# Four more polynomial exponential tiles, and other orders at the start and the end, in a soft-capped attention with a soft mixture of experts

## The chip, the cores and the metric

The kernel runs on one core of a Trainium2 chip. The time is that of the device, in microseconds (us), for one launch; 8 runs of the kernel before are at hand. A core has five engines with queues of their own: PE (TensorE, matrix products and transposes, results in PSUM), ACT (ScalarE, functions of one argument), DVE (VectorE, elementwise), POOL (GpSimd) and SP (SyncE, here only DMAs). Within an engine, instructions run in the order of its queue; between engines they wait on semaphores.

## What is computed

```python
scores = cap * tanh((q @ k.T) / 8 / cap)        # 8 x 12 heads, 448 x 448, head_dim 64, cap 30
attn = exp(scores - max) / (sum(...) + 1e-9)
x = (attn @ v), heads side by side              # 3584 tokens x 768

logits = x @ phi                                # 3584 x 32 slots
d = softmax of logits over the tokens           # dispatch
slot_input = d.T @ x                            # 32 x 768, 4 slots for each of 8 experts
slot_out[e] = relu(slot_input[e] @ w1[e]) @ w2[e]   # 768 -> 1024 -> 768
c = softmax of logits over the slots            # combine
out = c @ slot_out                              # 3584 x 768, float32
```

## The kernel before

**Attention.** A pair is two heads of one batch; there are 48, two to a quad. Seven key tiles `c` of a pair make 336 tiles, each a column block of 448 scores over 128 partitions. A chunk `j` is six of them (`CH`), so there are 56 chunks (`NCH`), seven to a batch. `qk_chunk` (L283) puts half a chunk's scores into one of two PSUM tiles `sc`; `tanh_chunk` (L295) turns them into `ex` (ACT); `exp_part` (L304) takes the exponential in place (ACT). Since the cap bounds the scores, no maximum is subtracted. `pv_first` and `pv_rest` (L371, L388) multiply with the values and a column of ones, in a single PSUM tile with tag `pv`, and `norm` (L355) divides by the sum: a reciprocal and a multiply on DVE, which write `xq` and release that PSUM tile.

**Tiles of the exponential on DVE.** For a chunk in `shared` (L318), `exp_chunk` (L307) leaves tile 0 out, and `poly_exp` (L325) computes it on DVE in five steps (a scale and shift to a fixed-point power of two, the whole part as exponent bits, two steps of a polynomial in the fraction, the product), numbered 0 to 4. `PARTS` says after which slot of which chunk each step is queued, by `j % 7`. All share one scratch tile, `work`.

**The order of the work** is written out by hand. `at(j, slot, f, ...)` puts a job into slot `a`, `b`, `c`, `d`, `e` or `r` of chunk `j`, and `run(j, slot)` (L584) calls them; a `<` or `>` puts a job ahead of or behind the others of its slot. The main loop (L611) queues, for each chunk: two tanh, the exponential of the chunk before, `pv_first`, slot a, the scores of a half chunk, slot b, `pv_rest` (slot r between its reciprocal and multiply), slot c, the other scores, slot d. `spare`, `fill` and `busy` are matrix products of ones without use, which keep PE busy; `FILL` (L525) places those of every batch. Transposes of q, k and x, logits and small sums share the one PSUM tile with tag `T`.

**Start.** `first_half` (L223) brings q and k of the first pair into place: a cast to bf16, PE transposes (`turn`) into PSUM banks `one` and `two`, and copies out, in the order of the list at L231. `boots` are the two PSUM tiles that `sc` later uses.

**End.** After the loop (L646 on) come the last two pairs, the last logits, and the slot sums `slT` (L708). `e_norm` (L450) adds the dispatch weights of a batch to `zacc` (PE, DVE); of the last batch it runs at L772 and gives the factor `rz` that `relu` (L743) needs. `layer1` (L732) makes a half of the hidden layer for four experts, `h_transp` (L749) turns it into `hpad`, which `clear_hpad` (L516) has cleared on POOL (it lies in the memory of `work`), and `layer2` (L763) makes one half (384 columns) of the slot outputs `so`. The output is 28 pieces of 128 rows. While the second half of layer 2 runs, `half_tile` (L788) writes the first half of pieces 0 to 9 (`NH`); afterwards it writes their second halves, and the other pieces go out whole, two pieces to a store (L832 on).

Of the kernel before, what the change touches and what calls it, by code (L numbers as in the profile page):

```python
# [36 lines left out]
def kernel(  # L37
# [171 lines left out]
    def first_pieces(h, jobs):  # L209

        for stage, nm, c0, c1, eng, bank, at0 in jobs:
            copy = act.copy if eng is act else dve.tensor_copy
            cols = slice(h * HP, h * HP + HP)
            if stage == "cast":
                copy(casts[nm, 0][:, c0:c1, cols],
                     raws[nm, 0][h][:, c0 * DH:c1 * DH].rearrange("p (c d) -> p c d", d=DH))
            elif stage == "turn":
                for c in range(c0, c1):
                    pe.transpose(bank[cols, at0 + c - c0, :], casts[nm, 0][:, c, cols], ident)
            else:  # L220
                copy(qkT[nm, 0][cols, c0:c1, :], bank[cols, at0:at0 + c1 - c0, :])

    def first_half(h):  # L223
        for nm in ("k", "q"):
            if h == 0:
                qkT[nm, 0] = qk.tile([P, NT, P], BF16, name=nm + "T", tag=nm + "T")
        one = psT.tile([P, 8, P], BF16, name="ps1", tag="T")
        two = psV.tile([P, NT, P], BF16, name="ps2", tag="pv")
        if h == 0:

            first_pieces(h, (("cast", "k", 0, CS, dve, None, 0), ("cast", "q", 0, 4, dve, None, 0),  # L231
                             ("cast", "q", 4, NT, act, None, 0), ("turn", "k", 0, CS, pe, two, 0),
                             ("copy", "k", 0, CS, dve, two, 0), ("turn", "q", 0, 4, pe, one, 0),
                             ("cast", "k", CS, NT, act, None, 0),
                             ("copy", "q", 0, 4, dve, one, 0), ("turn", "q", 4, NT, pe, two, CS),
                             ("copy", "q", 4, NT, act, two, CS),
                             ("turn", "k", CS, NT, pe, one, 4), ("copy", "k", CS, NT, dve, one, 4)))
# [66 lines left out]
    def exp_part(j, u0, u1):  # L304
        act.activation(exs[j][:, u0:u1, :], exs[j][:, u0:u1, :], ACT.Exp, scale=cap)  # L305

    def exp_chunk(j):  # L307
        exp_part(j, 1 if j in shared else 0, CH)

    PARTS = {0: ((0, "a", (0, 1)), (0, "c", (2, 3)), (1, "<b", (4,))),
# [5 lines left out]
    shared = [j for j in range(NCH - 2) if j % 7 in PARTS and j > 5] if cap < 50 else []  # L318

    lead = POW2[0] / FRAC ** 3  # L320
    p2, p1, p0 = (c / POW2[0] * FRAC ** (n + 1) for n, c in enumerate(POW2[1:]))
    halves16 = xe.bitcast(U16).rearrange("p (s two) -> p s two", two=2)
    frac, whole = halves16[:, :, 0], halves16[:, :, 1]

    def poly_exp(j, ops):  # L325
        t = exs[j][:, 0, :]
        steps = (
            lambda: dve.tensor_scalar(xe, t, cap * math.log2(math.e) * FRAC,  # L328
                                      (127 + math.log2(lead)) * FRAC, ALU.mult, ALU.add),
            lambda: dve.tensor_scalar(xb.bitcast(U16), whole, 7, None, ALU.logical_shift_left),  # L330
            lambda: dve.scalar_tensor_tensor(xp, frac, p2, frac, ALU.add, ALU.mult),  # L331
            lambda: dve.scalar_tensor_tensor(xp, xp, p1, frac, ALU.add, ALU.mult),  # L332
            lambda: dve.scalar_tensor_tensor(t, xp, p0, xb, ALU.add, ALU.mult))  # L333
        for n in ops:
            steps[n]()

    def pv_mms(pr, c0, c1, gs, dst):

        Q, h = divmod(pr, 2)
        for tail in (False, True):  # L340
            for c in range(c0, c1):
                j, u = divmod(place[pr, c], CH)
                for g in gs:
                    if (g == NF) != tail:
                        continue
                    for n in range(2 if tail else 1):
                        r = slice(n * HP, n * HP + HP) if tail else slice(0, P)
                        q0, s0 = g * P, 2 * (g - gs[0])
                        out_, v_ = (dst[r, s0, :], vbds[Q % 2][r, h, c, n * W:n * W + W]) \
                            if tail else (dst[:, s0:s0 + 2, :], vbds[Q % 2][:, h, c, :])  # L350
                        pe.matmul(out_, exs[j][r, u, q0:q0 + (HP if tail else P)], v_,  # L351
                                  start=(c == 0 and g == gs[0] < NF), stop=(c == NT - 1),
                                  skip_group_check=True)

    def norm(pr, s0, s1, pv, between=()):  # L355
        Q, h = divmod(pr, 2)
        rec = xs.tile([P, NT, 1], F32, name="rec", tag="rec", bufs=4)[:, 0:s1 - s0, :]
        dve.reciprocal(rec, pv[:, 0:s1 - s0, DH:W])  # L358
        for f, a in between:
            f(*a)  # L360
        dve.tensor_tensor(xq[Q][:, h, s0:s1, :], pv[:, 0:s1 - s0, 0:DH],  # L361
                          rec.to_broadcast([P, s1 - s0, DH]), op=ALU.mult)

    def xq_tile(pr):
        Q, h = divmod(pr, 2)
        if h == 0:
            xq[Q] = xs.tile([P, 2, NT, DH], BF16, name="xq", tag="xq")
# [143 lines left out]
    def at(j, slot, f, *a):  # L511
        if j < 0:
            j, slot = 0, "b"
        aux.setdefault((j, slot), []).append((f, a))
# [7 lines left out]

        busy(n, psV.tile([P, P], F32, name="junk", tag="pv"))

    FILL = ((3, "a", fill, 2), (4, "a", fill, 2), (5, "a", fill, 2), (6, "a", spare, 10), (6, "c", spare, 14), (7, "a", fill, 24), (8, "a", fill, 8), (9, "a", fill, 2))  # L525
    PER = 2 * NQB * NT // CH
    assert PER == 7 and NQB == 3

# [10 lines left out]
    for b in range(B):  # L539
# [20 lines left out]
        if b < B - 1:  # L560
# [9 lines left out]
    for j in shared:  # L570
        for dj, slot, ops in PARTS[j % 7]:
            at(j + dj, slot, poly_exp, j, ops)
    for n, job in enumerate(wjobs):
        at(1 + n * (NCH - 5) // len(wjobs), "b", *job)
    for j, slot, n in ((0, "a", 10), (0, "c", 10), (1, "b", 10), (1, "c", 8)):
        at(j, slot, spare, n)
    for j, slot, n in ((NCH - 6, "d", 8), (NCH - 4, "d", 8), (NCH - 2, "d", 12)):
        at(j, slot, spare, n)
    at(NCH - 1, "a", clear_hpad)
    at(0, "c", init_vbd, 0)  # L580
    at(1, "c", init_vbd, 1)
    at(0, "d", vcast, 0)
# [28 lines left out]
    for j in range(NCH):  # L611
# [31 lines left out]
        run(j, "c")  # L643
        qk_chunk(2 * j + 3)
        run(j, "d")
    assert not aux, aux.keys()  # L646
    last, hpad = NPAIR - 1, hpads[0]
    assert place[last, 0] == NTILE - NT and pair_at[NCH - 3] == last - 2
    CL = CS
    exp_part(NCH - 1, 0, CL)  # L650
    exp_part(NCH - 1, CL, CH - 1)
    exp_part(NCH - 1, CH - 1, CH)
    attp.close()
# [10 lines left out]
    pv2 = [bank([P, 4, W], name=f"pvl{half}") for half in range(2)]  # L664
    junk = bank([P, P], name="junk")
    xq_tile(last - 1)
    for half, gs in enumerate(halves):
        pv_mms(last - 1, 0, NT, gs, pvm[half])
        norm(last - 1, cuts[half], cuts[half + 1], pvm[half])
        if half == 0:  # L670
            logits(NQ - 2)
    for half, gs in enumerate(halves):
        pv_mms(last, 0, NT - CH + CL, gs, pv2[half])
    x_transp(last - 1)
    for half, gs in enumerate(halves):
        pv_mms(last, NT - CH + CL, NT - 1, gs, pv2[half])
# [30 lines left out]
        js = slice(3 * s, 3 * s + 3)  # L707
        dve.tensor_tensor(slT[:, js, :], sl_ps[:, js, :], slacc[:, js, :], op=ALU.add)  # L708
    e_rep(bl)
    busy(8)  # L710
    att.close()


# [27 lines left out]
        return i, half, hp  # L741

    def relu(i, half, hp):  # L743
        if half == 0:
            act.activation(hbs[i][:, 0:512], hp, ACT.Relu, scale=rz)
        else:
            dve.tensor_scalar(hbs[i][:, 512:1024], hp, rz, 0.0, ALU.mult, ALU.max)

    def h_transp(i):  # L749

# [18 lines left out]
                      start=(n0 == 0), stop=(n0 == len(blocks) - 4))  # L769

    first = [layer1(0, half) for half in range(2)]
    e_norm(B - 1)  # L772
    for hp in first:
        relu(*hp)
    relu(*layer1(1, 0))
# [30 lines left out]
            act.mul(ob, home, winv[:, bb, c:c + 1])  # L806
        store(n, half, half + 1, ob)

    NH = 10
    so = [wts.tile([P, HD], BF16, name=f"so{half}", tag="w1", bufs=E) for half in range(2)]  # L810
    n2 = len(blocks)
    for n0 in range(0, n2, 4):
        if n0 == n2 // 2 - 8:
            h_transp(1)
        layer2(n0, 0)
    act.copy(so[0], so_ps[0])
    done = 0
    for n0 in range(0, n2, 4):
        layer2(n0, 1)

        if n0 % 8 == 4 and n0 != n2 // 2 + 4 and done < NH:
            for eng in ("act", "dve") if n0 < n2 // 2 else ("act",):
                half_tile(done, 0, bank([P, HD], name="op0") if done else
                          [bank([P, HD // 2], name="op00") for _ in range(2)], eng)
                done += 1
    dve.tensor_copy(so[1], so_ps[1])
    assert done == NH
    mid.close()


# [64 lines left out]
```

## Time and profile before

| What | us |
|---|---|
| median of 8 runs | 305.44 (305.16 to 305.85) |
| the profiled execution: its time | 305.36 |
| the profiled execution: its span, first to last instruction or transfer | 303.6 |
| first tanh starts | 6.98 |
| last exponential of the attention is queued in one row | 252.95 to 256.53 |
| layer 1, first matmul | 261.54 |
| first store of the output is issued | 272.25 |
| last compute on an engine ends | about 293.2 |

The page of a profile gives the busy time of each engine, then the span in 40 equal slices with a digit for the busy share in each, then DMA queues, the chain of work that ended last, and the costliest groups of instructions. The timeline lists instructions with start and duration in us, engine, line, operation, out<-in with shapes, a count where several are merged, and in brackets the idle time before it and what ended that. The chain of waits goes back from the last instruction, each piece to what released it. The table of windows gives, for a stretch A:B in us, the busy time and count of PE, PEld (weight loads), DVE, ACT and POOL, then the granted PE clock, the share of the DMA engines and GB/s. PEclk is the clock granted to PE, in tenths of full speed.

### The profile page before, as it was taken

To read this page: it belongs to the slowest core of one execution; us is meant where nothing else is said; L and a number is where in the kernel's file an instruction comes from. 1 tells how busy PE (TensorE), PEld (TensorE's weight loads), DVE (VectorE), ACT (ScalarE), POOL (GpSimd) and SP (SyncE) were. 2 spreads that over 40 slices of the span, in tenths; PEclk is the share of its full clock that TensorE was granted. 3 is DMA by queue.
4 is the path that set the end of the run, shared out by engine and by line. 5 is a ranking of instruction groups with operands and counts; after the bars stand their busy time and mean duration, and the time that the engine had idled before them with its cause. 6 is when DMAs were issued, how large, how long until landed. Compare 5 with 4: busy or idle time off the path is not lost.

```text
span 303.6 us, 10776 instructions
## 1 busy us (share of the span) xinstructions
PE 267.1 (88%) x4746; PEld 184.9 (61%) x4746; DVE 228.7 (75%) x493; ACT 269.0 (89%) x209; POOL 136.6 (45%) x176
## 2 busy tenths in 40 slices
PE   8898888999899989998999899999999999998820
PEld 7675656766666666666667566666666677642400
DVE  3714589889988999899879998999899845236840
ACT  4999999999999999999999999999999998236730
POOL 4483554385439534943394439443932260000000
PEclk9999999999999999999999999999999999999995
DMA  7999999799999999999899999999999649929997
GB/s 258 208 203 206 203 180 209 143 206 202 233 195 201 199 232 202 202 203 232 151 152 223 229 228 185 202 231 222 167 203 232 183 124 369 372 86 330 393 412 312
DMA packets 57486, 67.72 MB, mean 223 GB/s; under 512 B 3808, under 2 KB 53600, under 8 KB 57440
## 3 DMA queue, kind: packets, MB, share of 16 engines
q0 software_dynamic: 42448, 35.31, 75.2%
q1 hardware_dynamic: 14704, 31.50, 29.4%
q8 instruction: 37, 0.61, 0.8%
q10 hardware_dynamic: 288, 0.23, 0.2%
q14 instruction: 9, 0.07, 0.1%
HBM read 91.32 MB, written 18.87 MB: 363 GB/s over the span
## 4 chain that ended last, share of the span: by engine, by line
ACT 63%; PE 22%; DVE 7%; issue 4%; DVEq 0%; POOL 0%; ACTq 0%
ACT ex L301 34%; ACT ex L305 26%; PE pv L351 4%; PE sc L292 2%; PE so_ps L766 2%; PE hp L738 2%; PE junk L597 2%; PE op L846 2%; ACT ob L855 1%; PE boot L597 1%; PE op L802 1%; DVE xq L361 1%; ACT E L441 1%; DVE work L332 1%; PE pvl L351 1%
## 5 line engine op out<-in xcount | busy, mean ns | idle before, releaser
L301 ACT ACTIVATE ex<-sc 128x1344 bf16<-128x1344 f32 (+1 forms) x113 | 164.4, 1729 | 0.8 <-PE sc L292 0.8
L305 ACT ACTIVATE ex<-ex 128x2240 bf16<-128x2240 bf16 (+4 forms) x58 | 148.7, 2600 | 0.1
L351 PE MATMUL pv<-vbd,ex 128*128 128x130 bf16 (+1 forms) x1610 | 94.4, 211 | 8.9 <-DVE xq L361 6.3
L351 PEld LDWEIGHTS <-ex 128*128 128x128 bf16 (+1 forms) x1680 | 75.9, 101 | 29.2 <-issue 6.6
L292 PE MATMUL sc<-qT,kT 64*64 64x448 bf16 x672 | 69.6, 359 | 5.4 <-ACT ex L301 3.5
L270 POOL CAST vbd<-vraw 64x896 bf16<-64x896 f32 x23 | 21.9, 954 | 64.8 <-PE pv L351 43.9
L447 POOL COPY e<-E 128x512 bf16<-128x512 bf16 x9 | 5.5, 609 | 68.3 <-ACT E L441 34.6
L292 PEld LDWEIGHTS <-kT 64*64 64x64 bf16 x672 | 25.3, 104 | 12.5 <-issue 9.2
L332 DVE SCALAR_TENSOR_TENSOR work<-work 128x448 f32<-128x448 f32 x41 | 29.8, 727 | 0.7
L361 DVE TENSOR_TENSOR xq<-pv,rec 128x448 bf16<-128x448 f32 x46 | 28.7, 624 | 1.6
L331 DVE SCALAR_TENSOR_TENSOR work<-work 128x448 f32<-128x448 uint16 x41 | 28.9, 705 | 0.0
L410 DVE COPY xT<-xps 128x448 bf16<-128x448 bf16 x47 | 18.3, 389 | 12.8 <-PE xps L404 12.4
L333 DVE SCALAR_TENSOR_TENSOR ex<-work 128x448 bf16<-128x448 f32 x41 | 26.5, 646 | 0.6
L271 POOL CAST vbd<-vraw 64x896 bf16<-64x896 f32 x23 | 24.7, 1073 | 1.4
L110 POOL DMA_DIRECT2D w1b<-in_moe_w_dram x32 | 24.6, 771 | 0.0
L597 PEld LDWEIGHTS <-ones 128*128 128x128 bf16 x333 | 20.3, 102 | 6.2 <-issue 4.3
L597 PE MATMUL junk<-ones 128*128 128x128 bf16 x297 | 21.4, 220 | 0.8 <-DVE xq L361 0.3
L328 DVE TENSOR_SCALAR work<-ex 128x448 int32<-128x448 bf16 x41 | 20.6, 503 | 1.9 <-ACT ex L301 0.9
L262 DVE COPY kT<-kps 128x896 bf16<-128x896 bf16 x23 | 14.3, 621 | 8.9 <-PE kps L260 8.6
L182 POOL DMA_DIRECT2D kb<-in_k_dram x22 | 16.1, 733 | 7.3 <-PE kps L260 6.5
L182 POOL DMA_DIRECT2D qb<-in_q_dram x22 | 16.2, 736 | 3.6 <-DMA kraw<-in_k_dram 3.6
L358 DVE RECIPROCAL rec<-pv 128x7 f32<-128x7 f32 x46 | 9.3, 202 | 10.6 <-PE pv L351 10.5
(119 smaller groups left out, 345.5 us busy)
## 6 DMA issues: line engine op xcount, KB each, us to landing
w1b<-in_moe_w_dram POOLq DMA_DIRECT2D x32, 384.0 KB, 8.9
vraw<-in_v_dram SPq DMA_DIRECT2D x23, 448.0 KB, 5.4
w2d<-in_moe_w_dram POOLq DMA_DIRECT2D x20, 384.0 KB, 9.2
w2t<-w2d SPq DMA_DIRECT2D x20, 384.0 KB, 5.0
out_dram<-ob SPq DMA_DIRECT2D x8, 768.0 KB, 6.9
qb<-in_q_dram POOLq DMA_DIRECT2D x22, 224.0 KB, 9.0
kb<-in_k_dram POOLq DMA_DIRECT2D x22, 224.0 KB, 7.8
w2b<-in_moe_w_dram POOLq DMA_DIRECT2D x12, 384.0 KB, 9.0
```

The lines of the kernel that those rows point to most:

```text
L110: pool.dma_start(out=w1b[e][:, js, fs], in_=w1r[:, e, js, fs])
L182: (sp if nm == "v" else pool).dma_start(out=t, in_=quad_ap(nm, Q))
L271: pool.tensor_copy(t[HP:P, :, :, DH + 1:VW - 1], raw[HP:P])
L292: pe.matmul(sc[cs, u, 0:S], qkT["k", Q][r, c, cs], qkT["q", Q][r, :, cs], start=True, stop=True)
L301: act.activation(exs[j][:, half * CS + u0:half * CS + u1, :], sc[:, u0:u1, 0:S], ACT.Tanh, scale=qk_scale / cap)
L305: act.activation(exs[j][:, u0:u1, :], exs[j][:, u0:u1, :], ACT.Exp, scale=cap)
L331: lambda: dve.scalar_tensor_tensor(xp, frac, p2, frac, ALU.add, ALU.mult),
L332: lambda: dve.scalar_tensor_tensor(xp, xp, p1, frac, ALU.add, ALU.mult),
L333: lambda: dve.scalar_tensor_tensor(t, xp, p0, xb, ALU.add, ALU.mult))
L351: pe.matmul(out_, exs[j][r, u, q0:q0 + (HP if tail else P)], v_, start=(c == 0 and g == gs[0] < NF), stop=(c == NT - 1), skip_group_check= ...
L361: dve.tensor_tensor(xq[Q][:, h, s0:s1, :], pv[:, 0:s1 - s0, 0:DH], rec.to_broadcast([P, s1 - s0, DH]), op=ALU.mult)
L597: pe.matmul(junk if home is None else home, by, by, start=True, stop=True)
```

## The change

Tile 0 of chunks 3, 4, 5 and 53 is added to those that DVE computes (`EXTRA`), and steps of chunks with `j % 7` of 0, 1 and 6, and of 50 to 52, are queued at other slots. Two fills of each batch are shortened. At the start q's chunks 4 to 6 are cast, turned and copied first, in a PSUM bank of their own (`three`, in `boots[1]`). At the end `clear_hpad` is queued later, the last `e_norm` goes ahead of layer 1 in place of four useless products, the last `relu` is split between ACT and DVE, the copy of `so[0]` likewise, and pieces 10 and 11 join the half tiles (their first halves after the copy of `so[1]` is queued). The slots `t0` to `t2` hold no job.

```diff
         if h == 0:
 
-            first_pieces(h, (("cast", "k", 0, CS, dve, None, 0), ("cast", "q", 0, 4, dve, None, 0),
-                             ("cast", "q", 4, NT, act, None, 0), ("turn", "k", 0, CS, pe, two, 0),
-                             ("copy", "k", 0, CS, dve, two, 0), ("turn", "q", 0, 4, pe, one, 0),
-                             ("cast", "k", CS, NT, act, None, 0),
-                             ("copy", "q", 0, 4, dve, one, 0), ("turn", "q", 4, NT, pe, two, CS),
-                             ("copy", "q", 4, NT, act, two, CS),
-                             ("turn", "k", CS, NT, pe, one, 4), ("copy", "k", CS, NT, dve, one, 4)))
+            three = boots[1][:, CS - 1, :].bitcast(BF16).rearrange("p (c q) -> p c q", q=P)
+            first_pieces(h, (("cast", "q", 4, NT, act, None, 0), ("cast", "k", 0, CS, dve, None, 0),
+                             ("cast", "q", 0, 4, dve, None, 0), ("turn", "q", 4, NT, pe, three, 0),
+                             ("turn", "k", 0, CS, pe, two, 0), ("copy", "q", 4, NT, act, three, 0),
+                             ("turn", "q", 0, 4, pe, one, 0), ("copy", "k", 0, CS, dve, two, 0),
+                             ("cast", "k", CS, NT, act, None, 0), ("copy", "q", 0, 4, dve, one, 0),
+                             ("turn", "k", CS, NT, pe, three, 3), ("copy", "k", CS, NT, dve, three, 3)))
...
     def exp_chunk(j):
-        exp_part(j, 1 if j in shared else 0, CH)
+        exp_part(j, len(shared.get(j, ())), CH)
...
-    PARTS = {0: ((0, "a", (0, 1)), (0, "c", (2, 3)), (1, "<b", (4,))),
-             1: ((0, "<d", (0,)), (0, ">d", (1, 2, 3)), (1, "<b", (4,))),
+    PARTS = {0: ((0, "a", (0,)), (0, "<b", (1,)), (0, "c", (2,)), (0, "<d", (3,)), (0, ">d", (4,))),
+             1: ((0, "<d", (0,)), (0, ">d", (1, 2, 3)), (1, "a", (4,))),
...
-             6: ((0, "a", (0,)), (0, "<d", (1,)), (0, ">d", (2, 3)), (1, "<b", (4,)))}
-    shared = [j for j in range(NCH - 2) if j % 7 in PARTS and j > 5] if cap < 50 else []
+             6: ((0, "<b", (0,)), (0, "c", (1, 2)), (0, "<d", (3,)), (1, "a", (4,)))}
+    EXTRA = {3: (((0, "a", (0,)), (0, ">b", (1,)), (0, "<d", (2, 3)), (1, "a", (4,)),),), 4: (((0, "a", (0,)), (0, ">d", (1, 2)), (1, "<b", (3,)), (1, "r", (4,)),),), 5: (((0, ">b", (0,)), (0, "<d", (1,)), (0, ">d", (2, 3)), (1, "r", (4,)),),), 50: (((0, "<d", (0,)), (0, ">d", (1, 2, 3)), (1, "a", (4,)),),), 51: (((0, "<b", (0,)), (0, ">b", (1,)), (0, ">d", (2,)), (1, ">b", (3, 4)),),), 52: (((0, "c", (0, 1)), (0, "<d", (2,)), (0, ">d", (3, 4)),),), 53: (((0, "<b", (0,)), (1, "a", (1,)), (1, "<b", (2,)), (1, "<d", (3,)), (1, ">d", (4,)),),)}
+    shared = {j: (PARTS[j % 7],) for j in range(6, NCH - 6) if j % 7 in PARTS}
+    shared.update(EXTRA)
...
-    FILL = ((3, "a", fill, 2), (4, "a", fill, 2), (5, "a", fill, 2), (6, "a", spare, 10), (6, "c", spare, 14), (7, "a", fill, 24), (8, "a", fill, 8), (9, "a", fill, 2))
+    FILL = ((3, "a", fill, 2), (4, "a", fill, 2), (5, "a", fill, 2), (6, "a", spare, 10), (6, "c", spare, 12), (7, "a", fill, 18), (8, "a", fill, 8), (9, "a", fill, 2))
...
-    at(NCH - 1, "a", clear_hpad)
...
     for half, gs in enumerate(halves):
         pv_mms(last, 0, NT - CH + CL, gs, pv2[half])
+    clear_hpad()
...
     e_rep(bl)
-    busy(8)
+    busy(4)
+    e_norm(bl)
...
     def relu(i, half, hp):
-        if half == 0:
-            act.activation(hbs[i][:, 0:512], hp, ACT.Relu, scale=rz)
-        else:
-            dve.tensor_scalar(hbs[i][:, 512:1024], hp, rz, 0.0, ALU.mult, ALU.max)
+        f0, f1, mid = 512 * half, 512 * half + 512, 512
+        if i == half == 1:
+            mid = f0 + 288
+        if f0 < mid:
+            f2 = min(f1, mid)
+            act.activation(hbs[i][:, f0:f2], hp[:, 0:f2 - f0], ACT.Relu, scale=rz)
+        if mid < f1:
+            f2 = max(f0, mid)
+            dve.tensor_scalar(hbs[i][:, f2:f1], hp[:, f2 - f0:512], rz, 0.0, ALU.mult, ALU.max)
...
     first = [layer1(0, half) for half in range(2)]
-    e_norm(B - 1)
...
-    NH = 10
+    NH, NHL = 12, 10
...
-    act.copy(so[0], so_ps[0])
+    HB = HD // 2
+    act.copy(so[0][:, 0:HB], so_ps[0][:, 0:HB])
+    dve.tensor_copy(so[0][:, HB:HD], so_ps[0][:, HB:HD])
...
-        if n0 % 8 == 4 and n0 != n2 // 2 + 4 and done < NH:
+        if n0 % 8 == 4 and n0 != n2 // 2 + 4 and done < NHL:
...
     dve.tensor_copy(so[1], so_ps[1])
-    assert done == NH
+    for done in range(NHL, NH):
+        half_tile(done, 0, bank([P, HD], name="op0"), "dve" if done % 2 else "act")
```

More of the change, by code (lines that the diff above doesn't have):

```diff
@@ L316 @@
              5: ((0, "a", (0,)), (0, "c", (1,)), (0, ">d", (2,)), (1, "a", (3,)), (1, "<b", (4,))),
[1 row of a table removed]
-    shared = [j for j in range(NCH - 2) if j % 7 in PARTS and j > 5] if cap < 50 else []
[1 row of a table added]
+    EXTRA = {3: (((0, "a", (0,)), (0, ">b", (1,)), (0, "<d", (2, 3)), (1, "a", (4,)),),), 4: (((0, "a", (0,)), (0, ">d", (1, 2)), (1, "<b", (3,)), (1, "r", (4,)),),), 5: (((0, ">b", (0,)), (0, "<d", (1,)), (0, ">d", (2, 3)), (1, "r", (4,)),),), 50: (((0, "<d", (0,)), (0, ">d", (1, 2, 3)), (1, "a", (4,)),),), 51: (((0, "<b", (0,)), (0, ">b", (1,)), (0, ">d", (2,)), (1, ">b", (3, 4)),),), 52: (((0, "c", (0, 1)), (0, "<d", (2,)), (0, ">d", (3, 4)),),), 53: (((0, "<b", (0,)), (1, "a", (1,)), (1, "<b", (2,)), (1, "<d", (3,)), (1, ">d", (4,)),),)}
+    shared = {j: (PARTS[j % 7],) for j in range(6, NCH - 6) if j % 7 in PARTS}
+    shared.update(EXTRA)
+    if cap >= 50:
+        shared = {}
     lead = POW2[0] / FRAC ** 3
@@ L323, with poly_exp @@
     frac, whole = halves16[:, :, 0], halves16[:, :, 1]
-    def poly_exp(j, ops):
-        t = exs[j][:, 0, :]
+    def poly_exp(j, u, ops):
+        t = exs[j][:, u, :]
         steps = (
@@ L569 @@
                 at(*when("es"), e_sums, b // 2)
-    for j in shared:
-        for dj, slot, ops in PARTS[j % 7]:
-            at(j + dj, slot, poly_exp, j, ops)
+    for j, tiles in shared.items():
+        for u, parts in enumerate(tiles):
+            for dj, slot, ops in parts:
+                at(j + dj, slot, poly_exp, j, u, ops)
     for n, job in enumerate(wjobs):
@@ L645 @@
         run(j, "d")
-    assert not aux, aux.keys()
-    last, hpad = NPAIR - 1, hpads[0]
+    last = NPAIR - 1
     assert place[last, 0] == NTILE - NT and pair_at[NCH - 3] == last - 2
     CL = CS
-    exp_part(NCH - 1, 0, CL)
+    exp_part(NCH - 1, len(shared.get(NCH - 1, ())), CL)
     exp_part(NCH - 1, CL, CH - 1)
@@ L666 @@
     xq_tile(last - 1)
+    run(NCH - 1, "t0")
     for half, gs in enumerate(halves):
@@ L669 @@
         norm(last - 1, cuts[half], cuts[half + 1], pvm[half])
+        run(NCH - 1, f"t{half + 1}")
         if half == 0:
@@ L673 @@
         pv_mms(last, 0, NT - CH + CL, gs, pv2[half])
+    clear_hpad()
+    assert not aux, aux.keys()
+    hpad = hpads[0]
     x_transp(last - 1)
```

## The prediction

> **What bounds the kernel now.** I read the page first (busy shares, then the slices), then ScalarE's timeline, then the chain of waits, then a table of windows over the output. The page puts two engines level and cannot choose between them:
>
> ```profile
> PE 267.1 (88%) x4746; PEld 184.9 (61%) x4746; DVE 228.7 (75%) x493; ACT 269.0 (89%) x209; POOL 136.6 (45%) x176
> ...
> DVE  3714589889988999899879998999899845236840
> ACT  4999999999999999999999999999999998236730
> ...
> PEclk9999999999999999999999999999999999999995
> ```
>
> DVE has free tenths in slices 2 to 5 and again from slice 32: at the edges of the attention. ScalarE's timeline chooses:
>
> ```profile
> 85.67 2.75 ACT L301 ACTIVATE ex<-sc 128x1344 bf16<-128x1344 f32 x2
> 88.01 0.60 ACT L441 ACTIVATE E<-lg 128x128 bf16<-128x128 f32 x1
> 88.21 2.36 ACT L305 ACTIVATE ex<-ex 128x2240 bf16<-128x2240 bf16 x1
> 90.17 2.76 ACT L301 ACTIVATE ex<-sc 128x1344 bf16<-128x1344 f32 x2
> 92.51 2.75 ACT L305 ACTIVATE ex<-ex 128x2688 bf16<-128x2688 bf16 x1
> 94.84 2.78 ACT L301 ACTIVATE ex<-sc 128x1344 bf16<-128x1344 f32 x2
> ```
>
> Read starts, not durations: 88.21 to 90.17 is 1.96 us for a five-tile exp, 92.51 to 94.84 is 2.33 for a six-tile one, and these distances stay the same from 9.54 to 252.95 us with no idle entry. ScalarE is never starved. Recorded durations grow through the trace (the five-tile exp: 2.16 us at 40, 3.00 at 241), so ACT's start stamps run up to about 1 us early against the other engines; its ends fit them.
>
> At the end PE takes over, by the chain of waits:
>
> ```profile
> 246.00 0.62 PE sc L292 x6
> ...
> 248.55 0.79 PE junk L597 x12
> 249.34 0.04 issue
> 249.39 0.84 PE pv L351 x12
> ...
> 264.32 0.27 PE zps L455 x4
> ...
> 268.67 0.29 PE hps L755 x8
> ...
> 270.88 0.49 ACT so L816
> ```
>
> The scores at 245.87 start when the tanh of 243.60 has ended (245.82). Behind them PE runs with next to no gap to the last matmul of layer 2. After that the output's DMA is the limit:
>
> ```profile
> 278.00:280.00 2.00, 1.43 (x7) 0.56 (x6) 1.74 (x4) 1.63 (x4) 0.00 (x0) 1.00 0.65 227
> 280.00:284.00 4.00, 3.71 (x22) 1.76 (x22) 3.42 (x6) 3.58 (x5) 0.61 (x1) 1.00 1.04 370
> 285.00:294.00 9.00, 4.08 (x21) 1.82 (x19) 6.15 (x8) 4.93 (x6) 0.00 (x0) 1.00 1.02 415
> ```
>
> The last two columns are the DMA share and GB/s: full, except for a hole at 278 to 280.
>
> **1. Exponential tiles.** `shared` grows from 41 to 45 chunks: 3, 4, 5 and 53 are new. Each makes one exp five tiles wide instead of six: 2.33 - 1.96 = 0.37 us of ScalarE. Three early ones: **-1.12 us**, if PE and DVE follow. DVE pays five steps each (0.39 + 0.39 + 0.62 + 0.62 + 0.62 = 2.64 us); in 20 to 40 us it is busy 9.0 of 20. In its new order chunk 3's first two steps fall between the copy of qT (ends 21.17) and the next reciprocal (23.23). Chunk 4's last step goes between a reciprocal and the multiply of xq at about 32 us and holds xq, and the PSUM tile pv that PE reuses, by 0.55 us; PE has over 1.5 us until the tanh that releases its next scores (34.27), so this costs nothing. Were that cover gone it would cost its 0.55.
>
> What covers PE's lateness is the time from the last scores to their tanh: 0.48 us at its smallest recorded place in the loop's second half (235.48 to 235.97), 1.3 with ACT's early stamps put right. A shorter exp takes 0.37 of it.
>
> The fourth (chunk 53) falls into PE's own stretch. Its exp ends at 249.33, pv starts at 249.39; 0.37 earlier, PE is still in the 12 junk matmuls (until 249.34). DVE also finishes this tile late: its last two steps follow the copy of lg (248.55), so near 249.75, while pv reads it fourth of the pair, near 249.9. Ends: +0.2 (tile late) to -0.37 (all passes); I take **-0.10**, by the nearest row, PE's 0.04 us wait at 249.34.
>
> **2. Reordered steps (parts 0, 1, 6).** Same instructions, so no DVE time. Part 6 starts later in its chunk and ends sooner, parts 0 and 1 end sooner; behind the moved steps stand the copies of kT, qT and xT and the reciprocals, for whose PSUM tiles PE waits. Cover: the 1.3 us above. Cost 0; ends -0.3 and +4 (third rival).
>
> **3. Fewer fills.** 2 + 6 junk matmuls less per batch, 8 x 0.055 = 0.44 us. PE waits for ScalarE at the next scores, so nothing is gained. PEclk stays full at 20 to 40 us, where PE is busy only 17.16 of 20; the cut takes about 1.5 points from over 90%. Cost 0.
>
> **4. Start.** Now PE turns k, then q's first four chunks; q's last three wait for DVE's copy of kT, and ScalarE's copy of them (5.66, 0.47 us) is the last thing before the scores:
>
> ```profile
> 4.90 0.35 DVE L221 COPY kT<-ps 64x384 bf16<-64x384 bf16 x1 [0.42 <-PE ps L219]
> ...
> 5.22 0.42 DVE L221 COPY qT<-ps 64x512 bf16<-64x512 bf16 x1
> ...
> 5.66 0.47 ACT L221 COPY qT<-ps 64x384 bf16<-64x384 bf16 x1 [0.34 <-DVE qT L221]
> ...
> 6.19 1.32 PE L292 MATMUL sc<-qT,kT 64*64 64x448 bf16 x12
> ```
>
> After: q's three turns come first, in a bank of their own. Their cast ends at 4.10, PE can start at about 4.15 and pays 0.107 us each (its early spacing), so k's turns begin near 4.47 instead of 4.33: DVE's two copies slip 0.13, qT ends at about 5.77. ScalarE's copy runs at 4.71 to 5.18; its cast of the rest of k then slips from 4.92 to 5.18 and ends at 5.58; PE turns that k by 5.86, ahead of the scores in its queue. Scores at 5.87 instead of 6.19: **-0.32**; ends 0 (k's cast or its DMA late) and -0.5. The second scores still wait for DVE's copy of k, ready at 6.53 as before, and reach 7.34; their tanh comes at 7.9. Hidden.
>
> **5. From slots to layer 2.** Four junk matmuls and the four zps matmuls (0.22 + 0.27 us) now fill the wait for slT, where eight junk took 0.55: hidden, as long as POOL's e4 (ends 261.09) is not late. DVE's zacc sum and reciprocal (0.16 us each) go with them into DVE's idle time before 264.6. The 0.27 between the layer-1 halves goes. The relus no longer wait for rz (4.6 us on ScalarE), but what is late next is PE itself, so this gives no more. The last relu (DVE, 267.75, 0.75) held the transposes until 268.60 though PE had been free since about 268.4; split at 288 columns it takes about 0.50 on ScalarE (between 0.42 for 192 columns and 0.58 for 384), which removes that 0.2. **-0.47**; ends -0.2 and -0.6. clear_hpad moves behind id32 on POOL and waits for DVE's last step; from about 249.8 plus 1.8 it still ends 14 us before the first write to hpad. so[0] in two halves: 0.48 becomes about 0.36 (0.32 and 0.42 are the rows of 192 columns): **-0.12**; ends 0 and -0.2.
>
> **6. Two more early half tiles.** Before, the store issued at 276.89 is followed by the next at 278.37, since all wait for so[1]. Tiles 10 and 11 need only so[0]: their stores go out at about 277.5 and 278.0 and fill the hole, worth (370 - 227) / 370 x 2.0 = 0.77 us of DMA. Their other halves are small stores too: two tiles (0.79 MB) at 370 instead of 415 GB/s are 0.23 more. **-0.54**; ends +0.23 and -0.77. SP issues four small stores for one large, at 0.49 each, inside the 0.53 that each moves. The Trainium skill speaks against this step: "Perfetto Trace Analysis", DMA Optimizations, says that transfers under 2 KB carry a large overhead each and should be merged, and these rows are 1,536 bytes. "DMA: Bandwidth & Descriptors", Bandwidth, gives 0.95 us for 64 KB and 6.15 for 1 MB; my estimate between them for 192 KB is 1.7 us, so four stores would cost 6.8 where 0.79 MB at 415 takes 1.9: +4.9, and the change would be slower. The trace has the very store at 0.53 us, because the next is under way before one lands; I sum with that.
>
> **Sum:** -1.12 - 0.10 - 0.32 - 0.47 - 0.12 - 0.54 = -2.67 us. The profiled execution took 305.36 (span 303.6 and 1.76 around it), so 302.69; the runs' median 305.44 stands 0.08 above it. I forecast **302.7 us**.
>
> **Rivals.** (a) Partly hidden: the hole at 278 stays or moves, and start and relu give half. For it: DVE gets one more multiply just when so[1]'s first tiles come. Against: tiles 10 and 11 wait for nothing. 305.36 - 1.12 - 0.16 - 0.24 = **303.8**. (b) ScalarE's saving is eaten because PE, at 93% in the loop, cannot follow shorter chunks. For it: PE is late by over half a microsecond at chunks 52 and 53. Against: PE waits for ScalarE in nearly every earlier chunk. It keeps 4 to 6: **304.0**. (c) Slower: in the steady loop a reordered DVE step stands before a copy that PE needs, its 1.25 us (two steps at the end of part 0) pass the cover of 1.3 less 0.37, and ScalarE idles in each of the seven batches. It decides from 0.38 us a batch (2.67 / 7); at 0.6 it gives 305.36 - 2.67 + 4.2 = **306.9**. For it: DVE is 91% busy there. Against: the steps end sooner, not later. (d) Gains and losses cancel: 305.4.
>
> **Chances.** Forecast 0.60 (its own range 302.0 to 303.4), (a) 0.16, (b) 0.10, (c) 0.08, (d) 0.06. A change under 0.2% (0.6 us) cannot be told from none. Faster 0.86, same 0.06, slower 0.08. The range 301.9 to 304.5 takes in (a) and (b) and leaves out (c) and (d).
>
> **What would show it.** Five-tile exps 45 instead of 41, ScalarE's start distances unchanged and without idle entries; first scores near 5.9; scores of the last chunk near 244.4; no zps between the hp groups; 278 to 280 less 2.7 at full DMA rate. An idle entry on ScalarE between 20 and 250 us, PEclk under 9 in mid-run, or a pv waiting for DVE's last step would make it wrong.

## The result

The median after the change is **303.1 us** (302.86 to 305.39, 11 runs, ten of them at 303.38 or less) against 305.5 in 31 runs of the kernel before on the same chip; the ratio is 0.9928, with a 95% interval of 0.9917 to 0.9939. The profiled execution took 303.07, 2.29 less than that of before, and its span 301.3 is shorter by the same 2.29. The first rows of the page after:

```profile
PE 264.7 (88%) x4686; PEld 182.3 (61%) x4686; DVE 237.9 (79%) x515; ACT 267.8 (89%) x211; POOL 136.1 (45%) x176
...
DVE  3728989898998999899879998999899964336840
...
PEclk9999999999999999999999999999999999999995
```

ACT and PE are level as before; DVE's new steps stand in slices 3 to 5, where it had room. PEclk stays full. The exponential that gained can be read in ScalarE's timeline, by starts:

```profile
25.95 2.11 ACT L305 ACTIVATE ex<-ex 128x2240 bf16<-128x2240 bf16 x1
27.91 2.51 ACT L301 ACTIVATE ex<-sc 128x1344 bf16<-128x1344 f32 x2
...
86.93 2.36 ACT L305 ACTIVATE ex<-ex 128x2240 bf16<-128x2240 bf16 x1
88.89 2.76 ACT L301 ACTIVATE ex<-sc 128x1344 bf16<-128x1344 f32 x2
```

The same place before:

```profile
26.09 2.48 ACT L305 ACTIVATE ex<-ex 128x2688 bf16<-128x2688 bf16 x1
28.42 2.51 ACT L301 ACTIVATE ex<-sc 128x1344 bf16<-128x1344 f32 x2
```

The first of the new five-tile exps starts at 25.95 and is followed after 1.96 us; before, this place took 2.33. At 86.93 the distance is still 1.96, at the six-tile exp of 91.23 it is 2.33, and no row from 7 to 252 us has an idle entry: ScalarE still sets the pace.

The chain of waits at the end of the attention and through the last layers:

```profile
247.21 0.79 PE junk L601 x12
...
248.04 0.84 PE pv L355 x12
...
260.03 0.16 PE zps L459 x4
260.19 4.00 PE hp L747 x72
...
269.11 0.33 ACT so L830
269.46 0.37 DVE so L831
```

The sum `zps` now stands ahead of `hp`. The two halves of the copy of so[0] follow one another: VectorE starts when ScalarE has ended. Then the table of windows over the output, 1.6 us earlier than the windows shown of before:

```profile
276.40:278.40 2.00, 1.63 (x7) 0.57 (x6) 1.74 (x4) 1.69 (x3) 0.00 (x0) 1.00 1.04 367
278.40:282.40 4.00, 3.74 (x22) 1.68 (x20) 3.16 (x6) 3.32 (x5) 0.61 (x1) 1.00 1.03 366
283.40:292.40 9.00, 4.23 (x27) 2.00 (x26) 6.00 (x7) 4.39 (x5) 0.00 (x0) 1.00 1.02 409
```

The hole (227 GB/s) is gone. By stretches of the two traces, in us:

| Stretch | before | after | difference | forecast |
|---|---|---|---|---|
| start of the span to first tanh | 6.979 | 6.852 | -0.13 | -0.32 |
| to the last chunk's first scores | 238.886 | 237.669 | -1.22 | -1.12 |
| to the last chunk's pv | 3.521 | 3.520 | 0.00 | -0.10 |
| to layer 1 (`hp`) | 12.157 | 12.080 | -0.08 | 0 |
| `hp` to the first `hps` | 4.381 | 4.000 | -0.38 | -0.27 |
| first to second `hps` | 2.675 | 2.675 | 0.00 | -0.20 |
| to the copy of so[0] | 2.278 | 2.314 | +0.04 | 0 |
| copy of so[0] to the first store | 1.374 | 1.522 | +0.15 | -0.12 |
| first store to last transfer | 29.652 | 29.169 | -0.48 | -0.54 |
| last transfer to end of span | 1.682 | 1.494 | -0.19 | 0 |
| sum | 303.585 | 301.295 | -2.29 | -2.67 |

### The profile page after: what moved, and what is told of

Its sections match the earlier page's. It is cut to its first block, busy times and chain, and to the rows that moved or that the text cites. A ratio compares the mean times of both kernels' runs of the same rounds, so it can differ in the third digit from the quotient of the medians.

```text
span 301.3 us, 10670 instructions
## 1 busy us (share of the span) xinstructions
PE 264.7 (88%) x4686; PEld 182.3 (61%) x4686; DVE 237.9 (79%) x515; ACT 267.8 (89%) x211; POOL 136.1 (45%) x176
## 4 chain that ended last, share of the span: by engine, by line
ACT 64%; PE 20%; DVE 8%; issue 4%; POOL 1%; DVEq 0%; ACTq 0%
ACT ex L301 35%; ACT ex L305 26%; PE pv L355 4%; PE sc L292 2%; PE so_ps L780 2%; PE hp L747 2%; DVE xq L365 1%; PE op L862 1%; ACT ob L871 1%; PE boot L601 1%; PE op L815 1%; ACT E L445 1%; POOL vbd L270 1%; DVE work L335 1%; PE junk L601 1%
## 5 line engine op out<-in xcount | busy, mean ns | idle before, releaser
L305 ACT ACTIVATE ex<-ex 128x2240 bf16<-128x2240 bf16 (+4 forms) x58 | 147.0, 2571 | 0.1
L292 PE MATMUL sc<-qT,kT 64*64 64x448 bf16 x672 | 68.7, 359 | 4.9 <-ACT ex L301 3.8
L336 DVE SCALAR_TENSOR_TENSOR work<-work 128x448 f32<-128x448 f32 x45 | 32.7, 727 | 0.8
L335 DVE SCALAR_TENSOR_TENSOR work<-work 128x448 f32<-128x448 uint16 x45 | 31.9, 710 | 0.0
L337 DVE SCALAR_TENSOR_TENSOR ex<-work 128x448 bf16<-128x448 f32 x45 | 29.0, 644 | 0.7
L601 PEld LDWEIGHTS <-ones 128*128 128x128 bf16 x315 | 19.3, 102 | 6.6 <-issue 4.3
L601 PE MATMUL junk<-ones 128*128 128x128 bf16 x279 | 20.4, 220 | 1.1 <-DVE xq L365 0.8
L334 DVE TENSOR_SCALAR work<-work 128x448 uint16<-128x448 uint16 x45 | 18.6, 414 | 0.5
```

The costliest lines, as they stand in the source:

```text
L292: pe.matmul(sc[cs, u, 0:S], qkT["k", Q][r, c, cs], qkT["q", Q][r, :, cs], start=True, stop=True)
L601: pe.matmul(junk if home is None else home, by, by, start=True, stop=True)
```

## The experiments

Each is one edit of the kernel after, unless it says otherwise. Times are medians; the kernel before took 305.85, 305.48 and 305.52 us on the chip in the three groups, in the order told here. It differs by 0.37 between them, and the intervals of `so_whole`, `nh10`, `start_old` and `zps_late` overlap or touch that of the kernel after: what these four are worth is read from the stretches of their traces, and the medians only agree in direction.

**First group: four parts of the change, one at a time.** `no_tiles` computes tile 0 of chunks 3, 4, 5 and 53 on ScalarE again, `no_53` only that of chunk 53:

```diff
-    EXTRA = {3: (...), 4: (...), 5: (...), 50: (...), 51: (...), 52: (...), 53: (...)}
+    EXTRA = {50: (...), 51: (...), 52: (...)}                                  # no_tiles
+    EXTRA = {3: (...), 4: (...), 5: (...), 50: (...), 51: (...), 52: (...)}    # no_53
```

> The changed kernel without the four new exponential tiles (3, 4, 5, 53); the reordered steps, the shorter fills, start and end stay. Theory A (ScalarE's stream sets the time until PE's last stretch): the scores of the last chunk come 3 x 0.375 = 1.12 us later than in the changed kernel, and the time is 1.1 us longer, 304.2. Theory B (each exponential tile is worth its 0.37 wherever it lies): 1.5 us longer, 304.6. Theory C (PE's pace sets the loop and the reordered steps brought the gain): no longer than the changed kernel, 303.1.

> The changed kernel with the tile of chunk 53 given back to ScalarE. Theory A (behind the last chunk's scores PE sets the end): nothing changes after them; first matmul of layer 1 and time as in the changed kernel within 0.1 us, 303.1. Theory B: 0.37 us longer, 303.5.

`no_tiles` took 304.23 (ratio 0.9951, 0.9937 to 0.9965), 1.13 over the kernel after; `no_53` took 303.12 (0.9915, 0.9901 to 0.9928). The two ran in one group and differ by 1.11, so the three early tiles give the whole 1.1, and the fourth nothing. The trace of `no_tiles` agrees: from 50 us on its exps start 1.12 later, counted from the first tanh, than in the kernel after (until the clock falls at 92 us; see the end). The last chunk's pv follows its scores by 3.52 us before, after and in `no_53` alike: the twelve junk matmuls stand between, whenever the exp ends.

`so_whole` copies so[0] in one piece again:

```diff
-    act.copy(so[0][:, 0:HB], so_ps[0][:, 0:HB])
-    dve.tensor_copy(so[0][:, HB:HD], so_ps[0][:, HB:HD])
+    act.copy(so[0], so_ps[0])
```

> The changed kernel with so[0] copied by ScalarE in one piece. Theory A (the two halves of the split copy run one behind the other, since DVE's half waits for ScalarE): last matmul of layer 2's first half to the first whole op matmul shrinks from 0.9 to about 0.75 us, and the first store comes 0.15 us earlier; time 302.9 to 303.0. Theory B (the split saves a third of the copy, as its shorter rows say): 0.1 us longer, 303.2.

It took 302.80 (0.9904, 0.9891 to 0.9918), and its copy to first store 1.374 instead of 1.522. The split costs 0.15: two serial copies of 0.32 and 0.36 us with a hand-over, 0.71 in all, for one of 0.48; 0.08 is won back, since the first of the two products of piece 0 is made earlier. (The median fell by 0.30, more than expected; the intervals touch.)

`nh10` takes back the two early half tiles:

```diff
-    NH, NHL = 12, 10
+    NH, NHL = 10, 10
```

> The changed kernel with ten early half pieces as before instead of twelve. Theory A (the two more fill the hole in the output's transfers): the hole of about 0.7 us between the store of the tenth half piece and the next comes back, and the time is about 0.5 us longer, 303.6. Theory B (small stores cost what merging would save, and the hole is hidden by the transfers behind it): no longer, or shorter by up to 0.2.

It took 303.90 (0.9942, 0.9928 to 0.9957), 0.8 over the kernel after, for an expected 0.5. Two terms in the trace: the hole is back (first store to last transfer 29.648), and behind the last transfer the span ends after 1.68 us instead of 1.49. There SP passes one wait after another on the stores, 0.06 us each: eight behind the last transfer in `nh10` and before, five in the kernel after.

**Second group: what was still open.** `start_old` has before's list of first pieces; `fills_old` has before's numbers of fills; `zps_late` has eight junk matmuls ahead of layer 1 again and `e_norm` between its halves; `tail_free` changes several places of the tail together.

> Only the order of the first pieces is put back; all else as after the change. Theory A (the new order of turns is worth something, but less than 0.32 us where the granted clock rises late, since the ten turns before the first scores run at half clock until then): first scores at 6.1 to 6.3 us if the clock rises near 5, later than after's 6.06 at a later rise; time 303.1 + 0.2 to 0.4, so 303.3 to 303.5. Rival (the order is worth nothing, the moment of the clock's rise alone sets the first scores): time 303.1 within 0.1, and first scores at the same clock rise as early as with the new order (5.65 to 5.8 for a rise before 4.2 us).

It took 303.38 (0.9938, 0.992 to 0.9955), 0.28 more than after. The granted clock rose at 6.70 us in its trace and at 5.68 in that of after, so the first scores (6.37 and 6.06) are not to be compared alone. With the new order, profiles with a rise at 3.40, 4.16, 5.10 and 6.17 have their first scores at 5.65, 5.81, 6.02 and 6.24 (another with a rise at 3.51 has 5.76, so 0.1 is scatter); the old order in before's trace had 6.19 with a rise at 4.95. So both matter: the order by some 0.2 at nearly the same rise, the rise by up to 0.6.

```diff
-    busy(4)
-    e_norm(bl)
+    busy(8)
...
     first = [layer1(0, half) for half in range(2)]
+    e_norm(B - 1)
```

> Only the place of the last batch's sum is put back: eight junk matmuls in the wait for slT, and zps, sum and reciprocal between the layer-1 halves. Theory A (the move is worth 0.44: 0.27 of zps, 0.11 because the first relu and so the transposes no longer wait for the reciprocal, 0.06 because the eight junk matmuls had held the layer-1 matmuls): layer 1 starts 1.38 to 1.40 us after the last slpl instead of 1.383 or so with 0.06 more, hp to hps 4.38 instead of 4.00, time 303.1 + 0.44 = 303.55. Rival (the prediction: only the 0.27 of PE): hp to hps 4.27, time 303.35.

303.50 (0.9939, 0.9927 to 0.9951): 0.40 more. `hp` to the first `hps` is 4.381 again, and layer 1 starts 1.449 after the last slot products begin, instead of 1.383. By these two stretches the move is worth 0.45, more than the 0.27 of its matmuls on PE.

```diff
-    ... (6, "c", spare, 12), (7, "a", fill, 18), (8, "a", fill, 8), ...
+    ... (6, "c", spare, 14), (7, "a", fill, 24), (8, "a", fill, 8), ...
```

> Only the fill matmuls are put back to 14 and 24 (8 more per batch, 0.44 us of PE in each of seven batches). Theory A (ScalarE sets the pace, fills are free both ways): last chunk's scores as many us behind the first as after the change (238.46), time 303.1 within 0.15. Rival 1 (the cut was needed, since PE must follow shorter exps): later by up to 7 x 0.44 = 3 us, at least 0.5. Rival 2 (the cut lets the granted clock fall now and then, which cost 0.9 us in one profile): the median is lower by 0.2 or more.

304.07 (0.9955, 0.994 to 0.997): 0.97 more. Theory A fell; rival 1 has the number, but the trace denies its reason: from the first scores to the last chunk's it takes 238.468 us, and in the kernel after 238.463. All of it lies in the output: first store to last transfer 30.10 instead of 29.17. The windows and SP's timeline of `fills_old` there, and its DMA packets by queue from 276.9 to 277.9 (count, MB, share of the time of the 16 DMA engines):

```profile
276.30:277.80 1.50, 1.31 (x5) 0.38 (x4) 1.24 (x3) 1.39 (x3) 0.00 (x0) 1.00 1.04 363
...
278.30:278.80 0.50, 0.46 (x3) 0.10 (x1) 0.45 (x2) 0.46 (x1) 0.00 (x0) 1.00 0.06 9
```

```profile
277.11 1.48 SPq L796 DMA_DIRECT2D out_dram<-obh  x1
```

```profile
q1 hardware_dynamic: 255, 0.35, 96.5%
q8 instruction: 1, 0.02, 6.4%
```

One store's issue lasts 1.48 us. Its counterpart in the kernel after, at the same place behind the first store, lasts 0.41:

```profile
277.40 0.41 SPq L796 DMA_DIRECT2D out_dram<-obh  x1
```

The pieces of output are written at the same distances from the first store in both traces, so no tile was late. Meanwhile the DMA runs dry (9 GB/s). The other thing there is queue q8, one packet of 16,384 bytes at 277.17: a load of instructions. Its 6.4% of 16 engines' one us is 1.0 us, where a packet of q1, which carries the stores, takes 0.06 on average; the two stores issued in that stretch landed 3.9 us after their issue, those of the kernel after 2.1. In every profile 36 or 37 such packets lie on q8, some 7.3 us apart on average. That they are PE's code is inferred from their number: PE has 4,686 matmuls and as many weight loads; 36 loads for 9,372 instructions are one per some 260. The Trainium skill ("Runtime: NRT & Kernel Launch", Instruction fetch mechanics) says that engines stream their code in blocks of 16 KiB, 256 instructions, and calls the crossing mostly hidden. In the kernel after, the last load comes at 269.31, ahead of the first store, and no other follows. With 56 matmuls and their weight loads more, PE is further on in its code at every moment: the last two loads come at 266.75 and 277.17, and the latter is among the stores.

`tail_free` copies so[0] and the last relu whole, cuts the junk, and queues chunk 53's steps earlier:

```diff
-    for j, slot, n in ((NCH - 6, "d", 8), (NCH - 4, "d", 8), (NCH - 2, "d", 12)):
+    for j, slot, n in ((NCH - 6, "d", 8), (NCH - 4, "d", 8), (NCH - 2, "d", 1)):
...
-    53: (((0, "<b", (0,)), (1, "a", (1,)), (1, "<b", (2,)), (1, "<d", (3,)), (1, ">d", (4,)),),)
+    53: (((0, "<b", (0,)), (1, "a", (1,)), (1, "<b", (2, 3)), (1, "<c", (4,)),),)
...
-        if i == half == 1:
-            mid = f0 + 288
```

> From after: so[0] copied whole by ScalarE, the last layer-1 relu whole again on VectorE, 1 junk matmul instead of 12 before the last pv, and the fourth tile's VectorE steps moved one or two slots earlier. Theory A (the fourth exponential tile's 0.37 us is hidden only by the 12 junk matmuls on PE; the relu split gave nothing; the split copy cost 0.15): first pv of the last chunk follows its scores by 3.15 us instead of 3.52; the two groups of hps stay 2.675 apart; time 303.1 - 0.37 - 0.15 = 302.6. Rival 1 (behind the junk VectorE or another wait takes over): distance stays 3.4 to 3.5 and the time is 302.8 to 302.95. Rival 2 (the relu split did help, as the prediction has it): hps groups 2.87 apart, time 302.8 at best. Rival 3 (without the junk the clock falls or a bank is not free): over 303.1.

303.39 (0.9933, 0.9921 to 0.9944): none of the four. Up to the first store all went as theory A has it: from the last chunk's first scores to the beginning of the last slot products 13.85 us instead of 14.22 (pv comes 0.61 earlier, 0.25 of which is lost again behind it), the two `hps` groups 2.675 apart, copy to first store 1.372. But the output took 29.81, and again one store's issue was long, 1.05 us at 270.38, with a load of code at 269.99.

**Third group: the load of code (theory C) against its rivals.** If the load is the cause, its place is set by the number of PE instructions ahead of it. Then 14 fills fewer should cost time, 126 more should cost none, and 14 put back should mend `tail_free`.

```diff
-    ... (6, "c", spare, 12), (7, "a", fill, 18), (8, "a", fill, 8), ...
+    ... (6, "c", spare, 14), (7, "a", fill, 24), (8, "a", fill, 18), ...    # fills_more
+    ... (6, "c", spare, 12), (7, "a", fill, 16), (8, "a", fill, 8), ...     # fills_less
+    ... (6, "c", spare, 14), (7, "a", fill, 18), (8, "a", fill, 8), ...     # tail_page: tail_free with this
```

> From after: 18 fill matmuls more per batch (2 and 6 as in the kernel before, and 10 more in another slot), 126 in all, close to the 128 matmuls (256 PE instructions with their weight loads, 16 KB) that lie between two of PE's code loads. Theory C (the 0.97 us of the old fills is no time of PE: PE's code load of 16 KB came at 277.17, among the small stores, held one issue on SP for 1.48 us instead of 0.40 and emptied the DMA; with 126 more it falls where it fell in after, ahead of the first store): last load at 269 to 270, first store to last transfer 29.1 to 29.3, time 303.1 within 0.2, faster than the kernel with 56 more. If PE's slack in the loop does not hold 1 us more, the distance from first to last scores grows over 238.47, and the output still takes 29.2. Rival (fills cost PE time that the shorter exps need): more fills, more time: 304.5 or over.

> From after: 14 fill matmuls fewer (18 to 16 in one slot, seven batches). Theory C (PE's code load): with 14 fewer the last load slips by over 1 us, to about 271, among the first stores, holds one issue on SP for about 1 us, and first store to last transfer becomes 29.7 to 30.2: time 303.6 to 304.0, slower with fewer instructions. Rival (fills cost PE time, or nothing): 303.1 or less, output 29.2.

> tail_free (so[0] whole, relu whole, 1 junk for 12, tile 53's steps earlier) with 14 matmuls put back as fills in the loop (12 to 14 in one slot, seven batches), so that PE's last code load falls ahead of the first store again. Theory C: no store's issue on SP over 0.45 us before the large ones, first store to last transfer 29.1 to 29.3 instead of 29.81, time 302.5 to 302.7 (303.1 - 0.37 for the fourth tile - 0.15 for the whole copy), the fastest of all. Rival (tail_free's output was longer for another reason: SP's third store waited for a slower tile): 303.2 to 303.4 again.

| Kernel | PE matmuls | load of code nearest the stores | first store issued | longest issue of a small store | first store to last transfer | time |
|---|---|---|---|---|---|---|
| before | 4746 | 277.24 | 272.25 | 0.41 | 29.65 | 305.5 |
| nh10 | 4686 | 269.80 | 270.91 | 0.42 | 29.65 | 303.90 |
| after | 4686 | 269.31 | 270.63 | 0.41 | 29.17 | 303.1 |
| fills_old | 4742 | 277.17 | 270.33 | 1.48 | 30.10 | 304.07 |
| fills_more | 4812 | 269.24 | 270.73 | 0.41 | 29.14 | 303.19 |
| fills_less | 4672 | 273.27 | 272.99 | 1.29 | 30.05 | 304.15 |
| tail_free | 4675 | 269.99 | 269.89 | 1.05 | 29.81 | 303.39 |
| tail_page | 4689 | 269.32 | 270.14 | 0.42 | 29.15 | **302.56** |

Fewer fills are slower, and 126 more are not told apart from the kernel after (0.09). Theory C held in all three. The traces bear it out on PE's own count. Matmuls and weight loads that PE has begun when the last load comes, in the table of windows from the start of the span on, for the kernel after, `fills_less` and `fills_old`:

```profile
0.00:269.31 269.31, 247.99 (x4558) 175.65 (x4558) 221.54 (x490) 253.52 (x190) 135.47 (x175) 1.00 1.09 211
0.00:273.27 273.27, 251.16 (x4557) 177.11 (x4557) 220.75 (x493) 254.60 (x191) 136.61 (x175) 0.99 1.07 207
0.00:277.17 277.17, 256.51 (x4689) 179.40 (x4690) 225.61 (x500) 258.40 (x199) 136.79 (x175) 1.00 1.08 212
```

The five kernels of the table with 36 loads have 4,557 to 4,562 matmuls behind them there, the three with 37 have 4,684 to 4,689, one load or some 127 matmuls further: the last load stands at one of these two places in PE's code, wherever that falls in time. (`fills_less` is 1.05 over the kernel after, a little above the expected range. In its profiled execution, at 306.31 the longest of its 22 runs, the granted clock also fell to a half for 6.83 us in mid-run; the stretch in the table lies behind that, at full clock. The other 21 took 304.67 or less.)

`tail_page` has the ratio 0.9908 (0.9896 to 0.9921) and beats both kernels by the medians, though its interval touches that of the kernel after and it is not told apart from `so_whole` (0.9904) by the ratios. Its chain of waits shows where the fourth tile's saving passes:

```profile
251.18 1.18 ACT ex L301
252.36 1.22 ACT ex L305
...
253.62 0.99 PE pvl L355 x18
```

With one junk matmul instead of twelve, pv follows the last scores after 0.97 us instead of 1.59, PE is ahead of ScalarE again, and the chain runs over ScalarE up to 253.6. In the kernel after it is PE's alone from 244.52 on. ScalarE's stream is 0.37 shorter with the fourth tile (`no_53` has its last exps 0.37 later), so the 0.37 gained is taken to be the tile's; a kernel with one junk matmul and without that tile was not run.

## Why the prediction was right, and where it was off

The forecast of 302.7 had -2.67; the trace shows -2.29. The mechanism held: three early tiles and the filled hole carry most of it. Two things were luck: terms too large and too small cancelled in part, and the shorter fills did something that the prediction did not think of.

- **Exponential tiles.** The three early ones measure 1.13 by `no_tiles` (1.22 by the stretch of the trace; 0.1 of that is scatter, for `nh10`, with the loop of the kernel after, has 238.561 from the first scores to the last chunk's where that has 238.463), for a forecast of 1.12. Reading starts and not durations, 2.33 against 1.96, gave it. The fourth's term, -0.10, measured 0. The prediction had the right obstacle, the twelve junk matmuls until 249.34, but these cover the whole 0.37, and PE's wait of 0.04 behind them, which the prediction took for its measure, stands in all these traces and did not shrink. Without eleven of them 0.37 came through.
- **Reordered steps.** No idle time on ScalarE appeared, so rival (c) (306.9) fell, and with it (b) (PE cannot follow, 304.0): the distances after the exps of chunks 3 to 5 all keep 1.96, and `fills_more`, with 126 matmuls more on PE, has its last scores no later than `nh10`. The reason given against (b), that PE waits for ScalarE in nearly every earlier chunk, says more than the trace of before: its waits list 12 for a tanh before scores, 3.5 us together.
- **Fewer fills, "Cost 0".** Right for the loop, where 56 matmuls more moved the last scores by nothing. The term looked only at PE's time. What the cut really did was to move a load of code away from the stores. Before, such a load came at 277.24, and cost nothing, because SP was waiting for so[1] just then: before and `nh10` (with and without the load) both take 29.65. With twelve half tiles the wait is gone, and the load costs 0.93 where the fills stay (30.10 against 29.17). So without the cut the half tiles would have been a loss of 0.45 in this stretch, and the result 304.07, near rival (a) (303.8), for a reason that it did not have. The cut was part of the change, so this did not happen; in this term the forecast came out right by luck.
- **Start, -0.32.** Measured -0.13 in the two traces, and 0.28 by `start_old`. qT ended at 6.01 instead of the forecast 5.77. Of these 0.24, 0.13 lie in PE's first turn, forecast for 4.15: it came at 4.28 in the profile after, as in all six others of the new order whose clock rose after 4.3 (products of `boot` run until then), and k's turns at 4.60 instead of 4.47. The other 0.11 is the clock: the working took before's rise, 4.95, for granted; in the profile after it came at 5.68, so all ten first turns ran at 0.107 us each.
- **From slots to layer 2, -0.47.** Measured -0.42: 0.38 and 0.08, less 0.04. The total is near, but its parts are not. The prediction said of the relus' wait for rz that PE is late next anyway, and gave it nothing; the trace and `zps_late` give the move 0.11 more than the 0.27 of zps. The split of the last relu, -0.20, gave 0. The prediction had PE free since about 268.4 and held by the relu until 268.60. Ahead of the second `hps`, at 268.67, the chain of before has no such gap:

```profile
265.99 0.29 PE hps L755 x8
266.28 1.41 PE hp L738 x24
267.69 0.98 PE so_ps L766 x24
```

  PE's own work fills the 2.68 us between the two groups (its ends are modelled, so some hundredths are open). And the split did not shorten the relu: its parts are serial, 0.50 us on ScalarE from 265.94 and then

```profile
266.48 0.45 DVE L761 TENSOR_SCALAR hb<-hp,rz 128x224 bf16<-128x224 f32 x1 [1.60 <-ACT hb L758]
```

  where the bracket names ScalarE as what ended VectorE's wait. The relu ends at 266.93 there, behind the start of the transposes at 266.80; in `tail_page`, in one piece, it ends 0.10 ahead of them; the groups of hps are 2.675 apart in both.
- **so[0] in two halves, -0.12.** Measured +0.15: here too the halves are serial. The prediction took the longer of two parallel halves, 0.36; it is 0.32 + 0.36 and a hand-over. Its ends were 0 and -0.20, so the sign was missed.
- **Half tiles, -0.54.** Measured -0.48, and -0.19 more in the waits behind the last transfer, which the sum did not have. The hole is filled (367 GB/s), so rival (a) fell with its reason. The choice of the trace's row over the skill's rule was right: four more stores of 192 KB cost nothing like the 4.9 us that the rule's price gave.

Summed up: the terms too large (start 0.19, fourth tile 0.10, relu 0.20, copy 0.27, half tiles 0.06) are 0.82, the terms too small (zps and layer 1 0.15, less what follows them; end waits 0.19; loop 0.10) are 0.44, and the difference is the 0.38 by which the forecast was low.

## What to carry to other kernels

Where the output's DMA sets the end, look in the DMA packets for the instruction queue before an instruction count is changed anywhere: a load of code among small stores cost 0.6 to 0.9 us here, and moving it by a few idle matmuls cost nothing. Two engines given halves of one PSUM tile did not work side by side; before such a split is priced as a maximum, look for a row where it was done, and price it as a sum otherwise. A saving on the pacing engine passes only where the engine behind it has a gap: take away what fills that gap together with it.

## What was not expected of the hardware

- **Loads of code and issues of stores.** Three profiles show an issue on SP of 1.05 to 1.48 us instead of 0.42 at most, with a load of 16 KB on q8 beside it (277.17, 273.27, 269.99), and the other five of the table show none: no load lay among the small stores there, or SP was waiting anyway. Nor do the five profiles outside the table, where the last load came 1.1 to 1.7 us ahead of the first store. That the place of the load decides is shown by the three kernels of the third group. The packet of code took 1.0 us and stores under way landed late; how that holds the next issue on SP is open. The skill's "mostly hidden" holds for PE in these traces (in the kernel after its only wait from 249 to 271 us, over four loads, is 0.3 us on VectorE), not for SP.
- **The moment of the clock's rise.** It lies between 3.40 and 6.70 us in the 13 profiles, a spread of 3.3. The Trainium skill ("TensorE: Matmul & The Clock Gate", What's actually happening) has a free-running window of about 3.4 us, which fits, and a scatter of 500 ns either way, which does not.
- **Half clock in mid-run.** In `no_tiles` PE was busy 2.10 of 3.40 us and then had half its clock for 3.41, though no single wait was longer than 1.30:

```profile
88.75:92.15 3.40, 2.10 (x51) 1.75 (x47) 3.15 (x4) 3.40 (x4) 3.34 (x5) 1.00 0.71 97
92.15:95.56 3.41, 3.41 (x48) 2.21 (x45) 1.40 (x3) 3.41 (x3) 3.41 (x6) 0.50 1.08 224
```

  In `fills_less` it was 1.89 of 3.43, with one wait of 1.44 for a DMA, and 6.83 us at half clock. In the kernel after, PE is busy 3.07 and 3.24 of the same two stretches. One profile each does not show that fewer fills make it likelier.
